# Converting the first four weight tiles by way of SBUF in an attention and feed-forward kernel

## The chip, the cores and the metric

The kernel runs on one core of a Trainium2 chip. The metric is device time in microseconds (us). The engines are TensorE (PE in the rows, with PEld for its weight loads), VectorE (DVE), ScalarE (ACT), GpSimd (POOL) and SyncE (SP), which here only issues transfers.

## What is computed

Attention over 2 batches x 8 heads with rotary position encoding, then two feed-forward layers on its output. In the reference, cut to what matters:

```
q_rot, k_rot = rotate(q), rotate(k)              # (2, 8, 576, 64)
attn = softmax(scale * q_rot @ k_rot^T)
x = (attn @ v) as (1152, 512)                    # tokens x model
h = max(x @ w_in, 0);  y = (h * h) @ w_out       # 512 -> 2048 -> 512
out = ((y @ w_a) * (y @ w_b)) @ w2_out           # 512 -> 1536 -> 512
```

The weights arrive as 64-bit floats and are turned into 32-bit values inside the kernel.

## The kernel before

The 16 heads are worked in 8 pairs. A pair is 9 score tiles (`emit_S`, L205): each is 128 rows of queries against 576 keys. VectorE takes the row maximum of a score tile (L214), ScalarE the exponential (L220), PE transposes the result (L275), and some steps later PE multiplies it with v (`av`, L312 and L317). There are two score tiles in PSUM, so PE can make one score tile while the one before is being read. Beside this, each pair rotates the q and k of the next pair (`prepare`, L154 to L157, on VectorE and GpSimd together) and moves them to their places with transfers from SyncE's queue (`sk`, L142). The result of a pair is scaled and split into a high and a low half (L330, L333, L334) into `xb`, three blocks of 384 tokens.

The feed-forward layers run as units. `unit1(f, n)` is twelve matmuls (`three`, L391 to L393, for four slices of the model dimension): high half of the weight with high half of x, high with low, low with high. The first twelve units need the w_in tiles 0 to 3, called i0 to i3 here; then come i4 and the w_out tiles o0 to o3.

`prep_weight` makes one weight tile out of 64-bit floats. A transfer brings `raw` (two buffers). ScalarE writes `cl` (L77, L78), VectorE works on it in place (L79, L80) and joins it with the low words of `raw` to `bits` (L81); ScalarE rounds `bits` to the high half (L83), and GpSimd subtracts to get the low half (L84). The tiles go round 14 buffers: the first ones of each round lie in the pool `wa`, which exists from the start, the others in the pool `wb`, which takes over memory that attention has given back. Before the change, `wa` holds three tiles, and each `cl` lies in PSUM, in the pool `mps` of the feed-forward stage. This pool takes over the banks of attention's pool `ps`:

```python
attn.close()
...
mps.append(ctx.enter_context(tc.tile_pool(name="mps", bufs=6, space=bass.MemoryType.PSUM, reuse_waits="tile")))
```

All eight banks are attention's until then. `prep_weight` is called in program order, after the last line of attention, but a scheduler orders each engine's instructions by their dependences and free buffers, so an instruction can stand earlier in an engine's queue than in the code if what it writes to is free.

Of the kernel before, what the change touches and what calls it, by code (L numbers as in the profile page):

```python
# [26 lines left out]
LT = 3  # L27
DM = 512
NWT = 14
NWA = 3  # L30


@with_exitstack
def attention_moe_moe2_kernel(ctx: ExitStack, tc: tile.TileContext, qk, rope, vm, vt, ident_in, sel_in, w_in, w_out, w_a, w_b, w2_out, out):
# [8 lines left out]
    tmp = ctx.enter_context(tc.tile_pool(name="tmp", bufs=1))  # L43
    wpools = [ctx.enter_context(tc.tile_pool(name="wa", bufs=NWA))]

# [16 lines left out]
    def prep_weight(key):  # L62
        st = raw.tile([P, DM], I64, tag="raw", name=f"raw_{key[0]}{key[1]}")
        nc.sync.dma_start(out=st, in_=src_of[key[0]][key[1]])
        w = wpools[int(len(W) % NWT >= NWA)].tile([P, 2, DM], F32R, tag="w", name=f"w_{key[0]}{key[1]}")
        W[key] = w
        words = st.bitcast(I32).rearrange("p (n two) -> p n two", two=2)
        low = words[:, :, 0]
        highf = st.bitcast(F32).rearrange("p (n two) -> p n two", two=2)[:, :, 1]
        bits = tmp.tile([P, DM], I32, tag="bits", bufs=2, name=f"bits_{key[0]}{key[1]}")  # L70
        if mps:
            cl = mps[0].tile([P, DM], F32, tag="cl", bufs=2, name=f"cl_{key[0]}{key[1]}")
        else:
            cl = tmp.tile([P, DM], F32, tag="cl", name=f"cl_{key[0]}{key[1]}")
        clb = cl.bitcast(I32)

        act.activation(cl, highf, AF.Copy, scale=REBIAS)  # L77
        act.activation(cl, cl, AF.Prelu, alpha=TURN)  # L78
        dve.tensor_scalar(out=cl, in0=cl, scalar1=-HI * TURN, scalar2=HI, op0=ALU.max, op1=ALU.min)  # L79
        dve.tensor_scalar(out=clb, in0=clb, scalar1=3, scalar2=None, op0=ALU.logical_shift_left)  # L80
        dve.scalar_tensor_tensor(out=bits, in0=low, scalar=29, in1=clb, op0=ALU.logical_shift_right, op1=ALU.bitwise_or)  # L81
        val = bits.bitcast(F32)
        act.copy(w[:, 0, :], val)  # L83
        pool.tensor_tensor(out=w[:, 1, :], in0=val, in1=w[:, 0, :].bitcast(F32), op=ALU.subtract)  # L84

    src_of = {"i": w_in, "o": w_out, "a": w_a, "b": w_b, "2": w2_out}
    W = {}

    mps = []
# [291 lines left out]
    gb = ctx.enter_context(tc.tile_pool(name="gb", bufs=1, reuse_waits="tile"))  # L381
    wpools.append(ctx.enter_context(tc.tile_pool(name="wb", bufs=NWT - NWA, reuse_waits="tile")))
    accp = ctx.enter_context(tc.tile_pool(name="accp", bufs=1, reuse_waits="tile"))
# [114 lines left out]
    for fn, *a in steps:  # L498
        if fn is unit1:
            keys = [("i", a[0])]  # L500
        elif fn is unit2:
            keys = [("a", a[0]), ("b", a[0])]
        else:
            keys = [("o" if fn is out1 else "2", a[0] * G + k) for k in range(G)]
        for key in keys:
            if key not in W:
                prep_weight(key)
        fn(*a)
# [66 lines left out]
```

## Time and profile before

| | |
|---|---|
| time, median of 3 runs | 620.53 us (620.43 to 620.54) |
| the profiled execution's own time | 620.49 us |
| its span, first to last instruction | 618.7 us |
| busy: PE, PEld | 584.4 us (94%), 521.7 us (84%) |
| busy: DVE, ACT, POOL | 333.9 (54%), 322.1 (52%), 255.2 us (41%) |
| attention | from the start to about 180 us |
| feed-forward layers | from about 186 us to the end |

Busy shares are averages over stages with different limits. The ends of matmuls are modelled, so a stretch in which PE is fully busy is one in which its starts follow without a gap, not one at its peak.

### The profile page before, as it was taken

Reading aid. Unit: us, or ns where it says so; the run is one execution under the profiler, and the core shown is the slowest. Engines: PE = TensorE matmul, PEld = TensorE weight load, DVE = VectorE, ACT = ScalarE, POOL = GpSimd, SP = SyncE. Lnnn points to the kernel's source line nnn. Section 1 sums busy time; section 2 is a strip of 40 time slices with the busy share of each in tenths; the row PEclk is TensorE's granted clock in tenths of the full one; section 3 lists DMA queues with packets and bytes.
Section 4 is the critical chain, followed back from the end, with each engine's and each line's share of the span. In section 5 each row is a group of like instructions: output and inputs, shape, how many; then the busy total and the mean of one; then the engine's idle time right before and its main releaser. Section 6 shows DMA issues by size and latency. Waiting matters only on the chain.

```text
span 618.7 us, 8930 instructions
## 1 busy us (share of the span) xinstructions
PE 584.4 (94%) x3368; PEld 521.7 (84%) x3368; DVE 333.9 (54%) x550; ACT 322.1 (52%) x685; POOL 255.2 (41%) x278
## 2 busy tenths in 40 slices
PE   0699999999968999999999999999999999999998
PEld 0567666776637999999999999999988999889986
DVE  5977667754434766777675376764440553221122
ACT  2577777766635877774682356564452653102200
POOL 4567655521214863672561334444331534202210
PEclk9999999999987999999999999999999999999999
DMA  7675765550003344444341222232320440000012
GB/s 231 186 198 140 210 181 157 116 115 4 17 1 136 137 137 136 137 137 137 117 133 57 68 69 103 79 126 77 123 75 1 136 136 1 0 1 1 1 52 102
DMA packets 20678, 61.41 MB, mean 99 GB/s; under 512 B 3337, under 2 KB 3721, under 8 KB 19739
## 3 DMA queue, kind: packets, MB, share of 16 engines
q1 hardware_dynamic: 20635, 60.85, 32.3%
q8 instruction: 26, 0.43, 0.3%
q14 instruction: 17, 0.14, 0.1%
HBM read 48.16 MB, written 2.36 MB: 82 GB/s over the span
## 4 chain that ended last, share of the span: by engine, by line
PE 91%; DVE 5%; ACT 1%; DMA 1%; issue 1%; POOL 0%; SPq 0%; DVEq 0%; ACTq 0%
PE s L205 8%; PE av L317 7%; PE h L393 6%; PE h L391 5%; PE h L392 5%; PE y L391 5%; PE y L392 5%; PE y L393 5%; PE t L275 5%; PE a L392 4%; PE b L392 4%; PE a L393 4%; PE b L393 4%; PE a L391 4%; PE b L391 4%; PE o L467 4%
## 5 line engine op out<-in xcount | busy, mean ns | idle before, releaser
L411 POOL TENSOR_TENSOR g<-v,g 128x384 fp32r<-128x384 f32 x84 | 85.3, 1018 | 136.7 <-ACT g L410 129.9
L205 PE MATMUL s<-sk 128*128 128x288 f32 x336 | 65.1, 322 | 20.5 <-DVE sk L183 15.0
L205 PEld LDWEIGHTS s<-sk 128*128 128x128 f32 x336 | 48.5, 195 | 40.3 <-ACT P L220 15.0
L410 ACT CAST g<-v 128x384 fp32r<-128x384 f32 x84 | 42.9, 510 | 58.7 <-DVE v L409 58.1
L391 PE MATMUL h<-x,w_i 128*128 128x384 f32 x192 | 65.5, 341 | 7.3 <-ACT w_i L83 7.3
L214 DVE TENSOR_REDUCE st<-s 128x1 f32<-128x576 f32 x72 | 53.6, 751 | 34.6 <-PE s L205 34.4
L393 PE MATMUL h<-x,w_i 128*128 128x384 f32 x192 | 65.5, 341 | 1.1 <-POOL w_i L84 1.1
L392 PE MATMUL h<-x,w_i 128*128 128x384 f32 x192 | 65.1, 339 | 0.0
L391 PE MATMUL y<-g,w_o 128*128 128x384 f32 x192 | 64.1, 334 | 0.0
L392 PE MATMUL y<-g,w_o 128*128 128x384 f32 x192 | 64.1, 334 | 0.0
L393 PE MATMUL y<-g,w_o 128*128 128x384 f32 x192 | 64.1, 334 | 0.0
L220 ACT ACTIVATE P<-s,st 128x576 f32<-128x576 f32 x72 | 53.6, 745 | 11.3 <-DVE st L214 11.1
L391 PE MATMUL a<-yb,w_a 128*128 128x384 f32 x144 | 48.1, 334 | 0.0
L393 PE MATMUL a<-yb,w_a 128*128 128x384 f32 x144 | 48.1, 334 | 0.0
L392 PE MATMUL a<-yb,w_a 128*128 128x384 f32 x144 | 48.1, 334 | 0.0
L392 PE MATMUL b<-yb,w_b 128*128 128x384 f32 x144 | 48.1, 334 | 0.0
L393 PE MATMUL b<-yb,w_b 128*128 128x384 f32 x144 | 48.1, 334 | 0.0
L391 PE MATMUL b<-yb,w_b 128*128 128x384 f32 x144 | 48.1, 334 | 0.0
L317 PE MATMUL av<-PT,V 128*64 128x384 f32 (+1 forms) x256 | 48.0, 425 | 0.0
L409 DVE TENSOR_TENSOR v<-b,s 128x384 f32<-128x384 f32 x36 | 19.9, 553 | 50.3 <-PE b L393 50.3
L275 PE MATMUL t<-ident,P 128*128 128x128 f32 x288 | 45.6, 280 | 1.1 <-DVE PT L260 0.8
L391 PEld LDWEIGHTS h<-x,w_i 128*128 128x128 f32 x192 | 36.9, 192 | 8.0 <-ACT w_i L83 8.0
(118 smaller groups left out, 1340.9 us busy)
## 6 DMA issues: line engine op xcount, KB each, us to landing
raw_i<-in_w_in SPq DMA_DIRECT2D x16, 512.0 KB, 3.3
raw_o<-in_w_out SPq DMA_DIRECT2D x16, 512.0 KB, 3.3
X<-in_qk SPq DMA_DIRECT2D x7, 1152.0 KB, 5.3
raw_a<-in_w_a SPq DMA_DIRECT2D x12, 512.0 KB, 3.2
raw_b<-in_w_b SPq DMA_DIRECT2D x12, 512.0 KB, 3.3
raw<-in_w_out SPq DMA_DIRECT2D x12, 512.0 KB, 3.4
sk<-hi_lo SPq DMA_DIRECT2D x14, 432.0 KB, 5.7
sk<-hi_lo SPq DMA_DIRECT2D x14, 288.0 KB, 5.9
```

Source lines behind the costliest of these rows:

```text
L205: pe.matmul(s[:, b, c:c + n], lhs, rhs, start=(m < 2), stop=(m >= len(mm) - len(cuts)), skip_group_check=(j == 8))
L214: dve.tensor_reduce(out=ST[p][:, 0, j:j + 1], in_=SP[i][:, :, 0:288], op=ALU.max, axis=AX.XY, negate=True)
L220: act.activation(pr[:, h, :].rearrange("p (b n) -> p b n", b=2), SP.pop(i)[:, :, 0:288], AF.Exp, bias=st[:, 0, j:j + 1], scale=1.0, accum_ ...
L275: pe.transpose(t[:, k * P:(k + 1) * P], flat[:, c0:c0 + P], ident)
L317: pe.matmul(AVT[p, r][half(h), 0:n], V[p][:, h, k, :], PT[p][:, h, k, q0:q0 + n], start=False, stop=(k == 3), skip_group_check=True)
L391: pe.matmul(dst, wh, mh, start=first, stop=False)
L392: pe.matmul(dst, wh, ml, start=False, stop=False)
L393: pe.matmul(dst, wl, mh, start=False, stop=last)
L409: dve.tensor_tensor(out=val, in0=src, in1=other, op=ALU.mult)
L410: act.copy(gt[:, 0, c], val)
L411: pool.tensor_tensor(out=gt[:, 1, c], in0=val, in1=gt[:, 0, c].bitcast(F32), op=ALU.subtract)
L467: pe.matmul(dst, gt[:, 1, c], w[:, 0, d], start=False, stop=(k == G - 1))
```

## The change

The pool `wa` gets four tiles in place of three (so `wb` gets ten in place of eleven), and while the first four tiles are made, `cl` is a tile of the SBUF pool `tmp`, with one buffer, in place of a PSUM tile. `W` has the new key in it already when the test is reached, so its length is 1 to 4 for i0 to i3. All later tiles use PSUM as before.

```diff
-NWA = 3
+NWA = 4
...
         bits = tmp.tile([P, DM], I32, tag="bits", bufs=2, name=f"bits_{key[0]}{key[1]}")
-        if mps:
+        if len(W) > NWA:
             cl = mps[0].tile([P, DM], F32, tag="cl", bufs=2, name=f"cl_{key[0]}{key[1]}")
         else:
             cl = tmp.tile([P, DM], F32, tag="cl", name=f"cl_{key[0]}{key[1]}")
```

With that, the four conversions move in the queues of the engines. On PE, at the end of attention and the start of the first unit (`av7` is the last pair's product, `h0_0` the first unit's result, in brackets what an instruction waits for), before (-) and now (+):

```order
 L250 MATMUL r7_1_1889<-rows7_1_1891,sel_78 128x64
 L317 MATMUL av7_1_1896<-PT7_1670,V7_1731 64x192 x5
-L391 MATMUL h0_0_1941<-x0_80,w_i0_1931 128x384 [waits Activation_49]
+L391 MATMUL h0_0_1941<-x0_80,w_i0_1931 128x384
 L392 MATMUL h0_0_1941<-x0_80,w_i0_1931 128x384
-L393 MATMUL h0_0_1941<-x0_80,w_i0_1931 128x384 [waits Pool_49]
+L393 MATMUL h0_0_1941<-x0_80,w_i0_1931 128x384
```

The matmuls stand where they stood; the waits for ScalarE's high half and GpSimd's low half of i0 are gone.

On ScalarE, where pair 2 ends and pair 3 begins (`P3_0` is the first exponential of pair 3, `cl_i0` belongs to tile i0):

```order
 L220 ACTIVATE P2_4_701,st2_497<-s26_657,st2_497 128x576
 L258 COPY xf1_1_800<-r1_1_689 128x192
+L77 ACTIVATE cl_i0_1933<-raw_i0_1929 128x512
 L258 COPY PT2_570<-t23_704 128x4x128
+L78 ACTIVATE cl_i0_1933<-cl_i0_1933 128x512
 L220 ACTIVATE P3_0_720,st3_719<-s27_696,st3_719 128x576
 L258 COPY PT2_570<-t24_723 128x4x128
```

The first two steps of tile i0 have moved from the end of attention to this place, ahead of pair 3's exponentials.

On VectorE, early in pair 4 (`s37` to `s39` are its second to fourth score tiles, `cl_i1` belongs to tile i1):

```order
 L214 TENSOR_REDUCE st4_941<-s37_936 128x1
+L260 COPY PT3_792<-t34_962 128x4x128
 L214 TENSOR_REDUCE st4_941<-s38_955 128x1
-L260 COPY PT3_792<-t34_962 128x4x128
+L79 TENSOR_SCALAR cl_i1_1965<-cl_i1_1965 128x512
+L260 COPY PT3_792<-t35_994 128x4x64
+L80 TENSOR_SCALAR cl_i1_1965<-cl_i1_1965 128x512
 L214 TENSOR_REDUCE st4_941<-s39_986 128x1
 L330 TENSOR_TENSOR xf2_1_1022<-av2_1_932,xf2_1_1022 128x192
-L260 COPY PT3_792<-t35_994 128x4x64
```

Two steps of tile i1 now stand between two row maxima, and two copies have moved up. Tile i2 stands likewise in pair 5, and tile i3 at the end of pair 5. On SyncE the loads of i2, i3, i4 and o0 have moved from behind attention's last load to places among the loads and moves of pairs 5 to 7.

## Rows read from the trace of the kernel before

**Rows 1.** Busy us and instructions of each engine by stretch, clock, DMA share, GB/s.
```profile
core 0: us, PE busy (x) PEld busy (x) DVE busy (x) ACT busy (x) POOL busy (x), PEclk, DMA share, GB/s
...
72.00:90.50 18.50, 18.50 (x129) 12.92 (x128) 12.86 (x24) 13.73 (x34) 11.53 (x14) 1.00 0.69 188
90.50:111.00 20.50, 20.12 (x129) 13.60 (x128) 16.25 (x23) 13.66 (x34) 13.45 (x16) 1.00 0.54 145
111.00:129.50 18.50, 18.26 (x127) 12.71 (x126) 12.21 (x24) 13.63 (x35) 8.21 (x15) 1.00 0.42 94
...
148.00:166.50 18.50, 18.50 (x129) 12.94 (x127) 10.29 (x21) 12.72 (x34) 3.25 (x12) 1.00 0.06 17
220.00:300.00 80.00, 80.00 (x463) 80.00 (x463) 54.20 (x89) 53.06 (x104) 41.52 (x37) 1.00 0.42 137
```

**Rows 2.** What PE waited for: us in total, times, longest us.
```profile
PE h L391 <- ACT w_i L83: 7.3, 2, 6.2
```

**Rows 3.** PE's timeline at the boundary (start, us, what, idle before), and its stretch.
```profile
179.07 1.19 PE L317 MATMUL av<-PT,V 128*64 128x192 f32 x10
186.47 0.69 PE L391 MATMUL h<-x,w_i 128*128 128x384 f32 x1 [6.21 <-ACT w_i L83]
...
188.31 0.52 PE L391 MATMUL h<-x,w_i 128*128 128x384 f32 x1
...
192.47 0.39 PE L392 MATMUL h<-x,w_i 128*128 128x384 f32 x1
...
195.16 0.45 PE L391 MATMUL h<-x,w_i 128*128 128x384 f32 x1 [1.09 <-ACT w_i L83]
...
198.74 0.45 PE L393 MATMUL h<-x,w_i 128*128 128x384 f32 x1
199.02 0.34 PE L391 MATMUL h<-x,w_i 128*128 128x384 f32 x1
...
186.50:198.80 12.30, 10.13 (x39) 8.80 (x39) 4.92 (x8) 6.13 (x12) 7.00 (x6) 0.75 0.46 154
```

**Rows 4.** Stretches before and after PE's idle time, columns as in rows 1.
```profile
178.00:180.30 2.30, 2.26 (x20) 1.40 (x19) 0.24 (x2) 0.92 (x3) 1.14 (x2) 1.00 0.00 0
...
189.00:191.00 2.00, 2.00 (x8) 2.00 (x7) 0.03 (x1) 1.21 (x2) 0.00 (x0) 0.50 0.44 174
```

**Rows 5.** The chain that ended last, in order of time, behind attention's end.
```profile
181.11 1.06 ACT cl_i L77 x2
```

**Rows 6.** Groups by form: busy us, mean ns of one, idle before and its releasers.
```profile
L77 ACT ACTIVATE cl_i<-raw_i 128x512 f32<-128x512 f32 x16 | 10.0, 632 | 7.1 <-DMA raw_i<-in_w_in 7.1
L78 ACT ACTIVATE cl_i<-cl_i 128x512 f32<-128x512 f32 x16 | 9.2, 581 | 0.3
L83 ACT CAST w_i<-bits_i 128x512 fp32r<-128x512 f32 x16 | 9.9, 617 | 6.9 <-DVE bits_i L81 6.7
L79 DVE TENSOR_SCALAR cl_i<-cl_i 128x512 f32<-128x512 f32 x16 | 11.0, 696 | 12.4 <-ACT cl_i L78 12.4
L81 DVE SCALAR_TENSOR_TENSOR bits_i<-raw_i,cl_i 128x512 int32<-128x512 int32 x16 | 10.8, 682 | 0.7
L84 POOL TENSOR_TENSOR w_i<-bits_i,w_i 128x512 fp32r<-128x512 f32 x16 | 20.5, 1286 | 27.1 <-ACT w_i L83 27.1
L154 POOL TENSOR_TENSOR X<-X,cs_rot 128x1152 f32<-128x1152 f32 x6 | 18.6, 3097 | 0.0
```

**Rows 7.** The row maximum on VectorE, columns as in rows 6.
```profile
L214 DVE TENSOR_REDUCE st<-s 128x1 f32<-128x576 f32 x72 | 53.6, 751 | 34.6 <-PE s L205 34.4
```

**Rows 8.** Timelines of DVE and POOL in pair 4.
```profile
91.36 2.51 DVE L155 TENSOR_TENSOR cs_rot<-X 128x576 f32<-128x576 f32 x1
93.79 1.37 DVE L234 TENSOR_SCALAR st<-st 128x3 f32<-128x3 f32 x1
...
90.63 2.62 POOL L154 TENSOR_TENSOR X<-X,cs_rot 128x1152 f32<-128x1152 f32 x1
93.33 1.81 POOL L155 TENSOR_TENSOR cs_rot<-X 128x576 f32<-128x576 f32 x1
```

## The prediction

> **What bounds the kernel now.** I read four views: the busy table cut by stage, the waits of the matmul engine PE, its timeline where attention ends and the feed-forward stage begins, and the other engines' rows in that place and in attention.
>
> The stage table shows PE without a gap in the attention pairs that nothing disturbs (18.50 us busy of 18.50, in the stretches 72 to 90.5 and 148 to 166.5) and in the feed-forward stage (80.00 of 80.00) [rows 1]. So a microsecond that PE loses inside either stage is a microsecond of the span, and one that another engine loses is not, as long as its queue stays ahead of PE. VectorE and ScalarE are busy 12.86 and 13.73 us of such an 18.5 us pair. The exception is pair 4, the stretch 90.5 to 111: it takes 20.50 us.
>
> PE's list of waits has one large entry outside the start-up: 7.3 us in two pieces for ScalarE's L83, the high half of a converted w_in tile [rows 2]. The timeline places them. The last attention matmul ends at 179.07 + 1.19 = 180.26 us; PE then sits idle for 6.21 us until 186.47, starts, runs slowly, stops again for 1.09 us before 195.16, and only from 199.02 on do its starts follow each other evenly [rows 3]. The granted clock is 1.00 (2.4 GHz) up to 180.30 and 0.50 (1.2 GHz) at 189 to 191, after the idle stretch [rows 4]. What PE waits for is a chain that begins only when attention's last copy is through: ScalarE starts L77 on the first tiles at 181.11 [rows 5], though their bytes were in SBUF long before; `cl` lies in a bank of the feed-forward stage's PSUM pool, and those banks are attention's until then.
>
> **What the change removes.** In the changed order the first projection matmul carries no wait at all, and it stands right behind the last attention matmul; the waits for tiles i0 to i3 are gone, because all four are converted in pairs 3 to 5. What remains before h1_0 is one wait on ScalarE, and all that ScalarE has before the conversions at this place is over by 181.11, while h1_0 starts twelve matmuls after 180.26.
>
> Its worth: the table counts 39 matmuls from the first one (186.47) to 198.74, so the start at 199.02 is the fortieth [rows 3]. At the feed-forward pace, 80.00 us / 463 = 0.1728 us each [rows 1], 39 of them take 6.74 us. Without the gap the fortieth starts at 180.26 + 6.74 = 187.00, that is 12.02 us sooner. In this sum are 6.21 and 1.09 us of idle time, and 1.91 us of low clock in the stretch 188.31 to 192.47 alone (13 starts at 4.16 / 13 = 0.32 us in place of 0.173); the other 2.8 us are the waits for the low halves and the slow first matmuls behind each stop. Nothing of it is given back later, as far as I see: PE is busy without a gap from there on [rows 1], and tiles i4 and o0 are now loaded ahead as well, so their conversions can begin at about 181, and the first one is needed after twelve units of twelve matmuls (180.26 + 144 x 0.1728 = 205.1). Bounds: 12.0 if the clock stays at 1.00, as it does as long as PE works [rows 1, 4]; 9.1 if some 20 matmuls still run at 0.32 instead of 0.173.
>
> **What it adds in attention.** The instructions are the same; they stand elsewhere. Each tile brings ScalarE L77, L78 and L83 (0.63 + 0.58 + 0.62 = 1.83 us), VectorE L79, L80 and L81 (0.70 + 0.70 + 0.68 = 2.08, with L80 taken as L79) and GpSimd L84 (1.29) [rows 6]. Pairs 3 and 4 take one tile each, pair 5 two. For pair 3 that is 15.6 us of ScalarE and 14.9 of VectorE in 18.5, so PE stays the bound by the totals. By place, VectorE's row maximum L214 has 34.4 us in which it waited for PE's scores over the 72 tiles, about half a microsecond each [rows 7]; one conversion instruction in front of it (0.6 to 0.7) is mostly taken up there, since PE has a second score tile to work on. In pair 3 the ScalarE row order shows L77 and L78 ahead of the first exponentials, 1.2 us; PE has transposes and `av` matmuls moved forward to fill that, and I put it at nothing (bounds 0 and 1.2). In pair 5 one tile falls where VectorE is free and the other delays one maximum: 0.3. Pair 4 is the one that runs late already, and there L79 and L80 both stand ahead of a maximum: I take one of the two, 0.7, with bounds of nothing and both plus a GpSimd wait, 1.4 + 2.6.
>
> The gain side has an unknown as well: pair 4's extra 2.0 us come from a collision that the new order may shift. VectorE's L155 at 91.36 takes 2.51 us and ends at 93.87, 0.62 us after GpSimd's L154 (90.63 + 2.62 = 93.25) ends; its tiny L234 at 93.79 takes 1.37 and ends with GpSimd's L155 (93.33 + 1.81 = 95.14) [rows 8]. If the shifted rows miss each other, 2.0 us come back; I do not count on it, because both still start from the same transfers.
>
> By these rows, then, VectorE and GpSimd shut each other out on some instructions over SBUF tiles, and this speaks against the change: with `cl` in SBUF, L79, L80 and L81 join that group. The Trainium skill, "SBUF — State Buffer", section "Who interferes with whom", states it as a rule: a VectorE instruction with at most one SBUF input and no two-port mode does not contend with GpSimd, one with two SBUF inputs or a two-port `tensor_scalar` does, and the loser blocks for the whole instruction. The rows above agree (2.51 and 1.37 us, both ending with GpSimd's work); no row here shows a large `tensor_scalar` from SBUF. What it would do is a rival below.
>
> SyncE: the loads of i2, i3, i4 and o0 move up into attention's queue, behind the pair loads and ahead of later `sk` moves. Each waits for an L81, two tiles back. The `sk` moves behind them belong to the next pair and start late in the current one, after its L81, so I cost this at nothing; if an L81 slipped by a whole pair, the moves and then the next pair's scores would slip too.
>
> **The sum.** The profiled execution: span 618.70, time 620.49, so 1.79 us lie around the span; the median of three is 620.53, no different. 620.49 - 12.0 + 0.7 + 0.3 = 609.5 us.
>
> **Rivals.**
> *The lock costs more than a microsecond.* GpSimd is busy 11.53, 13.45 and 8.21 us in pairs 3 to 5, 58% of 57.5 us [rows 1]. Twelve VectorE instructions, 58% of them hit, each waiting about 1.5 us (the 1.9 and 1.2 that the two rows lost): 10.4 us, and 8.3 of their own. VectorE's idle time there is 18.50 - 12.86, 20.50 - 16.25 and 18.50 - 12.21, 16.2 in all. So 2.5 us stick out, and unlucky places add as much: 2.5 to 6 on the path, 611 to 614.5, say 612.5. For it: pair 4. Against it: many of the new rows stand where GpSimd has only the short instructions of the softmax scale.
> *Slower than before.* The same lock with every hit on the longest kind, GpSimd's L154 at 3.10 us [rows 6]: 12 x 3.10 + 8.3 = 45.5 us against 16.2 idle, 29 on the path, 637. It decides from (16.2 + 12.0 - 8.3) / 12 = 1.66 us per instruction on; L154 runs once a pair, so three hits are possible, not twelve.
> *Attention gets shorter too.* Pair 4's collision goes away and nothing is paid: 620.49 - 12.0 - 2.0 = 606.5.
> *The gap is filled by another wait.* The change would not do what it says if h0_0 met a late `xb` tile or a late bank. The order shows no wait at it, and attention's copies are through by 181.11. With half of the 6.21 us left, and the 1.91 us of low clock behind it, 609.5 + 3.1 + 1.9 = 614.5; if all of it stays and attention pays, 621.5.
>
> **How the numbers follow.** Likeliest, 0.70: the gap closes and attention pays between nothing and two microseconds and a half, 609.5, own range 608.5 to 611. Lock, 0.14: 612.5. Shorter, 0.10: 606.5. Other wait, 0.03: 614.5, or 621.5 in a third of these. Slower, 0.03: 637. For eight in ten I go from 606.5 to 613.5. A measurement of this kernel can tell about 0.2% (1.2 us) from no change. Faster by more: 0.70 + 0.14 + 0.10 + 0.02 = 0.96; the same 0.01; slower 0.03.
>
> **What would show it.** In the profile after: PE's 6.21 us entry for ScalarE L83 gone, the first h matmul within 0.3 us of the last `av` one, the clock at 1.00 across it, 0.17 us starts from the first unit on. L77 to L84 for `cl_i` in three stretches between about 72 and 131. Pair periods of 18.5 us in pairs 3 and 5, and 20 to 22 in pair 4. I would be wrong if PE shows new waits for ScalarE L220 of more than 2 us in pairs 3 to 5, if L79 to L81 show durations well over 1 us beside GpSimd's L154, L155 or L157, or if the second to fourth unit wait for a bank.

## The result, and the profile after

| | before | after |
|---|---|---|
| time, median of 4 runs each | 620.48 us (619.85 to 620.54) | 613.94 us (613.54 to 614.29) |
| profiled execution's span | 618.70 us | 611.8 us |
| last attention matmul ends | 180.26 us | 184.10 + 1.19 = 185.29 us |
| fortieth feed-forward matmul starts | 199.02 us | 192.09 us |
| from there to the end of the span | 419.68 us | 419.71 us |

The medians differ by 6.5 us, where 11.0 were forecast. The recorded ratio is 0.9882, with a 95% interval of [0.9863, 0.9901]; on 620.5 us that is 7.3 us less, a time of 613.2; why it is not the ratio of the two medians (0.9895) is not on record. The predicted 609.5 us was 4.4 us too low by the medians; they put the result 0.4 us above the upper end of the range, 613.5, and the ratio puts it 0.3 us below.

The table splits the difference of the spans. From the end of attention to the fortieth feed-forward matmul it took 199.02 - 180.26 = 18.76 us and takes 192.09 - 185.29 = 6.80, so 11.96 us are won. Attention ends 5.03 us later. Behind the boundary 0.03 us are lost. -11.96 + 5.03 + 0.03 = -6.9.

The boundary in PE's timeline of the changed kernel answers to [rows 3] (start, us, what, idle before):

```profile
184.10 1.19 PE L317 MATMUL av<-PT,V 128*64 128x192 f32 x10
185.22 0.44 PE L391 MATMUL h<-x,w_i 128*128 128x384 f32 x1
185.50 0.34 PE L392 MATMUL h<-x,w_i 128*128 128x384 f32 x1
...
192.09 0.33 PE L391 MATMUL h<-x,w_i 128*128 128x384 f32 x1
```

Its stretch by engines answers to the last of [rows 3] and to [rows 4] (the granted clock is the third figure from the end):

```profile
185.30:191.90 6.60, 6.60 (x38) 6.60 (x39) 4.53 (x9) 4.30 (x10) 1.75 (x3) 1.00 0.00 0
```

The 6.21 us of idle time are gone, the starts follow each other at 0.17 us from the second matmul on, and the clock stays at 1.00. The boundary is as forecast. PE's whole list of waits in the changed kernel (us in total, times, longest) answers to [rows 2]:

```profile
PE s L205 <- DVE sk L183: 15.0, 1, 15.0
PE s L205 <- ACT P L220: 5.1, 2, 4.0
PE t L275 <- DVE PT L260: 2.2, 2, 1.3
PE r L250 <- DVE rows L260: 1.4, 2, 1.0
PE t L275 <- ACT PT L258: 0.2, 1, 0.2
```

No entry for a weight tile is left. But the list does not explain 5 us either: between 45 us and the end of attention PE waited 1.3 us for a copy and 0.5 for `rows`; the rest is the start-up.

So I cut attention into pairs, from the start of one pair's last score tile (the only one of ten matmuls) to the next one's, and looked at the matmuls of the `av` tile alone. Columns: stretch, its length, busy us and instructions of PE, of its weight loads and of VectorE, clock, DMA share, GB/s. Pairs 3 to 6 of the kernel before, a cut that [rows 1] do not have:

```profile
69.28:87.79 18.51, 6.51 (x38) 2.38 (x36) 0.90 (x2) 1.00 0.69 189
87.79:108.27 20.48, 8.20 (x38) 3.03 (x36) 0.91 (x2) 1.00 0.54 145
108.27:127.10 18.83, 6.51 (x38) 2.38 (x36) 0.91 (x2) 1.00 0.43 95
127.10:145.66 18.56, 6.50 (x38) 2.38 (x36) 0.91 (x2) 1.00 0.43 96
```

and of the changed kernel:

```profile
69.29:88.84 19.55, 7.92 (x38) 2.74 (x36) 0.92 (x2) 1.00 0.64 179
88.84:110.71 21.87, 8.68 (x38) 2.84 (x36) 0.91 (x2) 1.00 0.58 160
110.71:132.19 21.48, 9.05 (x38) 3.21 (x36) 0.92 (x2) 1.00 0.51 132
132.19:150.69 18.50, 6.50 (x37) 2.38 (x36) 0.91 (x2) 1.00 0.53 125
```

Pairs 3, 4 and 5 take 1.04, 1.39 and 2.65 us more. In the same pairs the same 38 `av` records take 1.41, 0.48 and 2.54 us more of PE. The clock is 1.00 in all of them, and nothing was added to PE.

The rows of the whole engines in the same stretches (busy us of PE, PEld, DVE, ACT and POOL) split the difference. Pairs 4 and 5 before, then after:

```profile
87.79:108.27 20.48, 20.10 (x129) 13.58 (x127) 16.14 (x23) 13.66 (x34) 12.06 (x15) 1.00 0.54 145
108.27:127.10 18.83, 18.59 (x130) 13.04 (x128) 13.32 (x23) 13.68 (x34) 9.80 (x14) 1.00 0.43 95
```

```profile
88.84:110.71 21.87, 20.57 (x130) 13.39 (x128) 17.24 (x26) 15.58 (x38) 12.66 (x15) 1.00 0.58 160
110.71:132.19 21.48, 21.03 (x130) 13.77 (x128) 17.74 (x26) 16.83 (x40) 14.57 (x16) 1.00 0.51 132
```

PE has no idle time in pair 3, before or after. Over the three pairs it is busy 61.15 us in place of 57.20 and idle 1.75 in place of 0.62. So of the 5.08 us, 3.95 are longer work of PE itself and 1.13 are waits.

PE's timeline shows what makes the work longer. The eight matmuls of one `av` tile half at 384 columns are four steps, in each the 64 columns of head 0 and then those of head 1 (L317). In the kernel before they stand in two runs of four (each such matmul leaves two records):

```profile
122.84 1.51 PE L317 MATMUL av<-PT,V 128*64 128x384 f32 x8
...
125.66 1.51 PE L317 MATMUL av<-PT,V 128*64 128x384 f32 x8
127.10 1.07 PE L205 MATMUL s<-sk 128*128 128x288 f32 x7
```

and at the same place of the changed kernel:

```profile
124.48 0.86 PE L317 MATMUL av<-PT,V 128*64 128x384 f32 x2
125.27 0.22 PE L242 MATMUL r<-ident,part 128*18 128x128 bf16 x1
...
127.01 1.50 PE L317 MATMUL av<-PT,V 128*64 128x384 f32 x6
...
129.60 0.86 PE L317 MATMUL av<-PT,V 128*64 128x384 f32 x2
130.39 0.44 PE L285 MATMUL tk<-ident,P 128*128 128x128 f32 x2
130.75 1.50 PE L317 MATMUL av<-PT,V 128*64 128x384 f32 x6
```

In pair 4 of the changed kernel a run of two stands by itself:

```profile
104.68 0.87 PE L317 MATMUL av<-PT,V 128*64 128x384 f32 x4
105.48 0.53 PE L205 MATMUL s<-sk 128*128 128x288 f32 x2
```

A run of four holds PE for 125.66 to 127.10, 1.44 us. One matmul alone holds it for 124.48 to 125.27, 0.79 us, a run of two for 0.80, and three hold it as long as four. The two heads' matmuls use different halves of the array's columns and run side by side if they follow each other; where a transpose or a score matmul stands between them, each takes the time of a pair. The Trainium skill, "TensorE: Matmul & The Clock Gate", section "Part 3: Packing small matmuls — row/col tiling", says that such matmuls run concurrently in one array; the runs of four agree, and the runs of one and three show when it does not come about.

From this came two theories of the 5 us. **Order theory:** the scheduler, given the conversions, has put PE's queue into another order that splits `av` steps, three more at 384 columns and three at 192 (one of each in pair 3, two of each in pair 5; pair 4 has no more unpaired matmuls than before, but its `av` matmuls stand in ten runs in place of eight); PE itself takes longer. **Lock theory**, a rival of the prediction: VectorE and GpSimd shut each other out around the conversions, and ScalarE and VectorE carry more, so PE waits.

### The profile page after: what moved, and what is told of

It reads as the page before. It is cut to its first block, busy times and chain, and to the rows that moved or that the text cites. A ratio compares the mean times of both kernels' runs of the same rounds, so it can differ in the third digit from the quotient of the medians.

```text
span 611.8 us, 8929 instructions
## 1 busy us (share of the span) xinstructions
PE 584.6 (96%) x3368; PEld 520.3 (85%) x3368; DVE 333.6 (55%) x550; ACT 321.4 (53%) x685; POOL 257.2 (42%) x278
## 4 chain that ended last, share of the span: by engine, by line
PE 92%; DVE 5%; DMA 1%; issue 1%; ACT 1%; SPq 0%; DVEq 0%; ACTq 0%
PE av L317 8%; PE s L205 7%; PE h L391 5%; PE y L391 5%; PE h L393 5%; PE h L392 5%; PE y L393 5%; PE y L392 5%; PE t L275 5%; PE a L391 4%; PE a L393 4%; PE b L391 4%; PE b L393 4%; PE a L392 4%; PE b L392 4%; PE o L467 4%
## 5 line engine op out<-in xcount | busy, mean ns | idle before, releaser
L391 PE MATMUL h<-x,w_i 128*128 128x384 f32 x192 | 64.2, 335 | 0.0
L392 PE MATMUL h<-x,w_i 128*128 128x384 f32 x192 | 64.1, 334 | 0.0
L393 PE MATMUL h<-x,w_i 128*128 128x384 f32 x192 | 64.1, 334 | 0.0
L220 ACT ACTIVATE P<-s,st 128x576 f32<-128x576 f32 x72 | 53.6, 745 | 13.2 <-DVE st L214 13.0
L317 PE MATMUL av<-PT,V 128*64 128x384 f32 (+1 forms) x256 | 52.4, 425 | 0.0
L467 PE MATMUL o<-w,g 128*128 128x512 f32 (+1 forms) x112 | 42.8, 382 | 0.0
```

Of the source, the lines that this page charges most:

```text
L220: act.activation(pr[:, h, :].rearrange("p (b n) -> p b n", b=2), SP.pop(i)[:, :, 0:288], AF.Exp, bias=st[:, 0, j:j + 1], scale=1.0, accum_ ...
L317: pe.matmul(AVT[p, r][half(h), 0:n], V[p][:, h, k, :], PT[p][:, h, k, q0:q0 + n], start=False, stop=(k == 3), skip_group_check=True)
L391: pe.matmul(dst, wh, mh, start=first, stop=False)
L392: pe.matmul(dst, wh, ml, start=False, stop=False)
L393: pe.matmul(dst, wl, mh, start=False, stop=last)
L467: pe.matmul(dst, gt[:, 1, c], w[:, 0, d], start=False, stop=(k == G - 1))
```

## The experiments

All are timed against the kernel before on the same chip, in 4 to 9 runs each; runs 1 to 4, 5 to 8, 9 to 11 and 12 were on four chips, so medians of different groups compare less well than ratios. Executions differ by up to 2.8 us in when the last score tile of pair 1 starts (48.7 to 51.5 us; runs 12 and 8, with the same order on PE, 48.8 and 51.2), so the table beside the times gives pair lengths.

**Runs 1 to 4: PE's order tied, the other queues free.** A wrapper notes PE's attention instructions as the program emits them, and edges that only fix the order of issue then tie them into a written order (the table is not shown).

```diff
-    act, dve, pool, pe = nc.scalar, nc.vector, nc.gpsimd, nc.tensor
+    act, dve, pool, pe = nc.scalar, nc.vector, nc.gpsimd, InOrder(nc.tensor)
...
+    pe.tie(tc, ORDER)
+    pe = nc.tensor
     attn.close()
```

Run 1, kernel before with the changed kernel's PE order:

> The kernel before, with PE's attention instructions tied by issue-order edges into the order that they have in the changed kernel. The conversions stay at the boundary. Order theory (PE's new order splits the two heads' 64-column av matmuls into runs of odd length, and an unpaired one costs a whole slot: 0.64 us at 384 columns, 0.32 at 192; three more of each): attention ends about 3 us later, 620.5 + 3.2 = 623.7 us. Lock theory (VectorE and GpSimd shut each other out on the conversions, and the loads on VectorE and ScalarE do the rest): no conversion stands in attention, so 620.5 within half a microsecond.

Run 2, changed kernel with the PE order of before:

> The changed kernel, with PE's attention instructions tied into the order that they have in the kernel before; the conversions stay in attention (pairs 3 and 4). Order theory: about 3 us come back, 613.9 - 3.2 = 610.7 us. Lock theory: nothing comes back, 613.9 or more, since the conversions now crowd pair 4.

Run 3, kernel before, heads paired:

> The kernel before, with PE's own attention order, except that the first head's av matmul of each step is put off to stand right ahead of the second head's. Order theory: the kernel before has 5 wasted slots of 384 columns and 6 of 192, 5 x 0.64 + 6 x 0.32 = 5.1 us; where PE is not the bound (pairs 0, 1, 4) some is lost, so 4 to 5: about 616 us. Lock theory: 620.5, the order of these matmuls costs nothing.

PE's queue in the kernel before (-) and paired (+), at the first `av` tile (... stands for other operations):

```
-L317 MATMUL av_0_390<-PT_189,V_226 64x384
...
-L317 MATMUL av_0_390<-PT_189,V_226 64x384
+L317 MATMUL av_0_390<-PT_189,V_226 64x384 x2
...
-L317 MATMUL av_0_390<-PT_189,V_226 64x384
...
-L317 MATMUL av_0_390<-PT_189,V_226 64x384
+L317 MATMUL av_0_390<-PT_189,V_226 64x384 x2
```

Run 4, changed kernel, heads paired:

> The changed kernel with PE's own order and every av step paired in the same way; the conversions stay in attention. Order theory: 8 wasted slots of 384 columns and 9 of 192, 8 x 0.64 + 9 x 0.32 = 8.0 us at the most; with some lost to waits 607 to 608 us. Lock theory: 613.9.

**Runs 5 and 6.** Run 2 turned out unclear: with PE tied, the scheduler moved the conversions too, and three of the four fell into pairs 3 and 4. So from here on all engines' attention parts are tied, as the last step of the program, and only what is named differs.

```diff
         fn(*a)
+    tie(tc, ORDER)
...
+def tie(tc, order):
+    made = {i.name: i for i in tc.nc.cur_bb.bb.instructions}
+    for runs in order.values():
+        names = [f"I-{a + k}" for a, n in runs for k in range(n)]
+        for before, after in zip(names, names[1:]):
+            tc.add_manual_dep(made[after], before, mybir.DependencyInfo(mybir.DependencyClass.NoSync, mybir.DependencyReason.DATA), reason="order")
```

Run 5, the changed kernel with PE alone in the old order:

> The changed kernel with every engine's attention part tied: ScalarE, VectorE, GpSimd and SyncE in the changed kernel's own order, PE alone in the order of the kernel before. The conversions stand exactly where the change put them. Order theory: the 3.7 us that the order alone cost in the first run come back, 613.9 - 3.7 = 610.2 us, with pair periods of about 18.5, 21.4 and 19.3 us in pairs 3 to 5. Lock theory: 613.9, since nothing on VectorE, ScalarE or GpSimd has changed.

Run 6, the same with PE in the changed kernel's order, each first-head matmul moved down to its partner as in run 3:

> The changed kernel with the same ties, PE in its own order but each first-head av matmul put off to the second head's. Order theory: an unpaired av matmul costs 0.79 us at 384 columns (its slot and the restart behind it) and 0.39 at 192; 8 and 9 of them are wasted, 8 x 0.79 + 9 x 0.39 = 9.8 us, 604 us if no other engine becomes the bound, 607 to 610 if the other engines' orders keep part of it. Lock theory: 613.9.

**Runs 7 and 8: the conversions two pairs later.**

VectorE's queue in pair 6, against the kernel before:

```
 L214 TENSOR_REDUCE st_1387<-s_1401 128x1
+L79 TENSOR_SCALAR cl_i_1933<-cl_i_1933 128x512
+L80 TENSOR_SCALAR cl_i_1933<-cl_i_1933 128x512
 L260 COPY PT_1236<-t_1408 128x4x128
 L214 TENSOR_REDUCE st_1387<-s_1432 128x1
+L81 SCALAR_TENSOR_TENSOR bits_i_1932<-raw_i_1929,cl_i_1933 128x512
```

> The changed kernel with PE, ScalarE, VectorE and GpSimd tied into the order of the kernel before, and the four conversions put into pairs 6 and 7, two a pair, where GpSimd has no rotation to do (3.25 us busy of 18.5) and VectorE and ScalarE have 8.2 and 5.8 us free. Order theory: attention takes what it took before and the boundary gap is closed, 620.5 - 12.0 = 608.5 us, at most 0.5 more. Lock theory: the load stays, 3.66 us of ScalarE and about 3.0 of VectorE in each pair, but no GpSimd work to collide with, so 609 to 611.

> The same with PE's av matmuls paired in the order of before. Order theory: the kernel before wastes 5 slots of 384 columns and 6 of 192, 5 x 0.79 + 6 x 0.39 = 6.3 us; 608.5 - 6.3 = 602.2 us if the other engines follow, 604 to 607 if they keep part of it. Lock theory: as the run before, 609 to 611.

**Run 9: four splits, no conversion.** PE's queue in one of the four places, before (-) and now (+):

```
-L275 MATMUL t_1511<-ident,P_1_1437 128x128 x4
-L317 MATMUL av_0_1502<-PT_1236,V_1297 64x384 x4
+L275 MATMUL t_1511<-ident,P_1_1437 128x128 x3
+L317 MATMUL av_0_1502<-PT_1236,V_1297 64x384
+L275 MATMUL t_1511<-ident,P_1_1437 128x128
+L317 MATMUL av_0_1502<-PT_1236,V_1297 64x384 x3
```

> The kernel before with every engine's attention part tied to its own order, and in four places of pairs 6 and 7, where nothing else disturbs, one transpose put between the two heads' first av matmul of a run of four (384 columns). No work is added and no conversion stands near. Order theory: each place costs one slot and one restart, 4 x 0.79 = 3.2 us, in pairs 6 and 7 alone: 620.7 + 3.2 = 623.9 us. Lock theory: 620.7, the order of these matmuls is free.

**Runs 10 and 11: GpSimd's L84 moved.** GpSimd's queue at the start of pair 4's rotation and behind its end:

```
 L157 TENSOR_TENSOR hi_lo<-cs_rot,hi_lo 128x576
-L84 TENSOR_TENSOR w_i_1931<-bits_i_1932,w_i_1931 128x512
 L334 TENSOR_TENSOR x_80<-xf_0_898,x_80 128x384
 L154 TENSOR_TENSOR X_1175<-X_1175,cs_rot 128x2x576
...
 L157 TENSOR_TENSOR hi_lo<-cs_rot,hi_lo 128x576
+L84 TENSOR_TENSOR w_i_1931<-bits_i_1932,w_i_1931 128x512
```

> The fifth run's kernel (changed kernel, PE in the order of before), with the low-half subtractions L84 of tiles i0, i1 and i2 put behind the rotation's last GpSimd instruction L157 of their pair in place of ahead of its L154. VectorE, ScalarE and PE keep their orders. The fifth run paid 2.1 us in pair 4 and 1.0 in pair 5 over the kernel before. If GpSimd's L84 ahead of the rotation makes the VectorE instructions L154 and L155 wait (2.2 and 2.7 us in place of 1.2 and 0.7), most of that comes back: 612.0 - 2 = 610 us. If it is the plain load on VectorE and ScalarE, nothing: 612.0.

> The sixth run's kernel (changed kernel with paired av matmuls, 606.9 us) with the same three L84 moved. If the lock ahead of the rotation is what is left: pairs 4 and 5 fall from 20.9 and 19.7 towards 19 us, 604.5 to 605.5 us. If the load is: 606.9.

**Run 12: run 3 with the other queues held.** PE's order as in run 3, tied as in run 5.

> The third run again (kernel before, av matmuls paired), now with ScalarE, VectorE, GpSimd and SyncE tied to the order of the kernel before, so that PE's order is all that changes. The third run gave 2 us where 4 to 5 were expected, with new waits in pairs 2, 3 and 5. If those came from the other engines' queues, which the scheduler had rearranged: about what pairing gave between the seventh and the eighth run by pairs (1.1 in pair 2, 0.6 in pair 4, 0.2 in pair 5, 1.7 behind pair 7), 620.6 - 3.6 = 617.0 us. If pairing itself makes PE wait there: 619.4 as in the third run.

What was measured (ratio to the kernel before on the run's own chip with its 95% interval; lengths of pairs 2 to 7, and from the last score tile of pair 7 to the end of attention, of the profiled execution):

| | median us | ratio | 2 | 3 | 4 | 5 | 6 | 7 | end |
|---|---|---|---|---|---|---|---|---|---|
| before | 620.48 | | 19.49 | 18.51 | 20.48 | 18.83 | 18.56 | 18.55 | 16.05 |
| after | 613.94 | 0.9882 | 19.49 | 19.55 | 21.87 | 21.48 | 18.50 | 18.56 | 16.04 |
| 1 before, new PE order, rest free | 625.00 | 1.0054 [1.0035, 1.0073] | 19.49 | 19.55 | 20.96 | 20.98 | 18.51 | 18.55 | 16.04 |
| 2 after, old PE order, rest free | 613.61 | 0.9873 [0.9856, 0.9889] | 19.48 | 20.97 | 23.25 | 19.05 | 18.56 | 18.56 | 16.05 |
| 3 before, paired, rest free | 619.41 | 0.9978 [0.9961, 0.9995] | 19.84 | 19.89 | 18.46 | 20.06 | 18.56 | 18.55 | 14.34 |
| 4 after, paired, rest free | 612.00 | 0.9842 [0.9826, 0.9858] | 19.79 | 19.96 | 20.82 | 20.39 | 18.51 | 18.54 | 14.34 |
| 5 after, old PE order | 612.00 | 0.9860 [0.9845, 0.9875] | 19.50 | 18.82 | 22.54 | 19.79 | 18.54 | 18.56 | 16.04 |
| 6 after, paired | 606.86 | 0.9775 [0.9758, 0.9791] | 18.38 | 18.34 | 20.92 | 19.72 | 18.50 | 18.55 | 14.33 |
| 7 conversions late | 610.05 | 0.9821 [0.9804, 0.9837] | 19.49 | 18.50 | 20.47 | 18.83 | 18.54 | 19.09 | 16.04 |
| 8 late and paired | 605.97 | 0.9757 [0.9736, 0.9778] | 18.38 | 18.50 | 19.90 | 18.63 | 18.56 | 19.06 | 14.34 |
| 9 before, four splits | 624.92 | 1.0065 [1.0042, 1.0087] | 19.48 | 18.50 | 20.48 | 18.83 | 20.42 | 20.42 | 16.04 |
| 10 as 5, L84 moved | 609.90 | 0.9818 [0.9797, 0.9840] | 19.49 | 18.85 | 21.68 | 18.85 | 18.56 | 18.55 | 16.04 |
| 11 as 6, L84 moved | 604.50 | 0.9736 [0.9712, 0.9759] | 18.37 | 18.35 | 20.11 | 19.39 | 18.49 | 18.56 | 14.33 |
| 12 before, paired | 616.79 | 0.9936 [0.9905, 0.9966] | 18.38 | 18.51 | 19.90 | 18.65 | 18.54 | 18.56 | 14.33 |

The ties themselves cost nothing that shows: runs 7 and 9, tied into the order of before, repeat its pairs 2 to 5 to 0.02 us.

*Order is a cost of its own: runs 1 and 9.* Run 1 has no conversion in attention, and its pairs 3 to 5 take 1.04, 0.48 and 2.15 us more than before, 3.67 in all. Its `av` rows are those of the changed kernel (same columns):

```profile
70.20:89.75 19.55, 7.93 (x38) 2.74 (x36) 0.92 (x2) 1.00 0.65 179
89.75:110.71 20.96, 8.67 (x38) 2.84 (x36) 0.91 (x2) 1.00 0.54 142
110.71:131.69 20.98, 9.06 (x38) 3.21 (x36) 0.92 (x2) 1.00 0.38 86
```

Run 9 sets the price. Pairs 6 and 7, which take 18.5 to 18.6 us wherever nothing is put into them, grow to 20.42 with two splits each: 0.93 us a split, a little over the 0.79 expected. Its `av` rows for these two pairs, and one of the places in its timeline:

```profile
128.20:148.62 20.42, 8.21 (x38) 2.74 (x36) 0.91 (x2) 1.00 0.38 87
148.62:169.04 20.42, 8.21 (x37) 2.73 (x36) 0.91 (x2) 1.00 0.06 16
```

```profile
142.38 0.86 PE L317 MATMUL av<-PT,V 128*64 128x384 f32 x2
143.17 0.33 PE L275 MATMUL t<-ident,P 128*128 128x128 f32 x1
143.43 1.50 PE L317 MATMUL av<-PT,V 128*64 128x384 f32 x6
```

In run 1 the queues of ScalarE and VectorE moved too, but PE is busy 61.06 us in the three pairs, 3.86 more than before, and idle 0.43, no more than before: the time is PE's own. The lock theory expected nothing in either run. As the only cause it falls.

*But the conversions cost something too: run 5.* With PE in its old order, pairs 3 to 5 still take 0.31, 2.06 and 0.96 us more than before, 3.33 in all; the order theory as the only cause falls as well. Run 5 keeps ScalarE, VectorE and GpSimd in the changed kernel's order, so these 3.33 us are the price of the conversions together with queues that were arranged for another order of PE. PE's order 3.67 and this 3.33 make 7.0, where the change paid 1.04 + 1.39 + 2.65 = 5.08: the two overlap by 1.9 us. A likely reason is that a VectorE that is late costs nothing while PE is busy with its own extra slots; PE idles 3.34 us in these pairs of run 5, and 1.75 in the changed kernel. In pair 4 the two together even cost less than the second alone (1.39 and 2.06). So run 5 got 1.75 us of pair length back (1.9 by the medians), not the 3.7 expected.

*What in the conversions: runs 5 and 10.* VectorE, GpSimd, ScalarE and PE early in pair 4 of run 5, in order of start:

```profile
89.64 1.28 POOL L84 TENSOR_TENSOR w_i<-bits_i,w_i 128x512 fp32r<-128x512 f32 x1 [0.76 <-ACT w_i L83]
89.95 2.19 DVE L154 TENSOR_TENSOR X<-X,cs_rot 128x1152 f32<-128x1152 f32 x1
90.88 2.12 POOL L334 TENSOR_TENSOR x<-xf,x 128x384 fp32r<-128x384 f32 x1
...
92.96 2.64 POOL L154 TENSOR_TENSOR X<-X,cs_rot 128x1152 f32<-128x1152 f32 x1
...
93.52 2.69 DVE L155 TENSOR_TENSOR cs_rot<-X 128x576 f32<-128x576 f32 x1
...
98.41 0.74 ACT L220 ACTIVATE P<-s,st 128x576 f32<-128x576 f32 x1 [2.40 <-DVE st L214]
...
99.29 0.79 PE L205 MATMUL s<-sk 128*128 128x288 f32 x4 [1.24 <-ACT P L220]
```

and VectorE and GpSimd at the same place of run 10, where L84 stands behind the rotation:

```profile
88.94 1.35 DVE L154 TENSOR_TENSOR X<-X,cs_rot 128x1152 f32<-128x1152 f32 x1
89.65 1.50 POOL L334 TENSOR_TENSOR x<-xf,x 128x384 fp32r<-128x384 f32 x1 [1.78 <-ACT x L333]
...
91.11 2.63 POOL L154 TENSOR_TENSOR X<-X,cs_rot 128x1152 f32<-128x1152 f32 x1
91.84 2.51 DVE L155 TENSOR_TENSOR cs_rot<-X 128x576 f32<-128x576 f32 x1
```

In run 5 the low-half subtraction of tile i0 runs when the rotation of the next pair begins. VectorE's L154 takes 2.19 us beside it, in place of 1.35, and GpSimd reaches its own L154 at 92.96; the row maxima behind come late, ScalarE's exponential waits 2.40 us, and PE then 1.24 (1.59 and 0.39 in run 10). Moving three L84 gives pair 4 back 0.86 us and pair 5 0.94. The medians, 612.00 and 609.90 on two chips, say 2.1, as the lock half of the expectation had it.

1.56 us stay with the conversions, 1.20 of them in pair 4. No run was made to split them, but two records speak against the plain load on VectorE or ScalarE. Run 7 has two tiles in pair 6, with the queues otherwise as before, and that pair takes 18.54 us (though there is no rotation beside them). And in pair 4 of run 10, PE's longest wait is for an exponential that stands behind a copy of ScalarE:

```profile
98.69 0.37 ACT L258 COPY PT<-t 128x256 f32<-128x256 f32 x1 [1.05 <-PE t L275]
...
98.96 0.75 ACT L220 ACTIVATE P<-s,st 128x576 f32<-128x576 f32 x1
...
99.85 0.80 PE L205 MATMUL s<-sk 128*128 128x288 f32 x4 [0.62 <-ACT P L220]
```

Its row maximum had been ready since 97.77. In the kernel before the exponential (97.04) comes first and the copy (98.20) after it; the scheduler swapped them when the conversions moved, and run 10 keeps the swap. A second wait, 0.43 us for `rows` at 104.41, follows an L81 of 1.19 us (0.68 for tile i0) beside GpSimd's L157. Together they are 1.05 of the 1.20 us. So the order of ScalarE's queue looks like a third part of the cost, which neither theory had; a run with the two put back was not made.

*Runs 2 to 4, 6 and 12.* Run 3 was expected at 616 and came at 619.4. Run 12, the same PE order with the other queues held, gives 616.79 (617.0 expected): the shortfall of run 3 was the scheduler's rearrangement of the other engines, not the pairing. Run 4 against run 6 (the same PE edit, other queues free or held, 612.00 and 606.86) shows the same. Run 2 is undecided for that reason. Run 6, at 606.86, lies at the end of its 607 to 610 us for order theory and far from the lock theory's 613.9. It shares all queues but PE's with the changed kernel, and pairs 3 to 5 take 58.98 us in it in place of 62.90: pairing alone takes 3.92 us out of them.

*A version that beats both.* Run 11, with the conversions in their new places, the heads paired and L84 behind the rotation, takes 604.50 us (604.5 to 605.5 expected, though pairs 4 and 5 did not come down to 19); run 8, with conversions in pairs 6 and 7, 605.97 (604 to 607 expected if the other engines keep part). Much of what pairing gains was there before the change: in run 12, 1.1 us in pair 2 and 1.7 behind pair 7. Run 7 confirms 12 us for the boundary with attention nearly untouched: pair 7 alone pays, 0.54 us, and the time is 610.05 where 608.5 was expected from the order theory and 609 to 611 from the lock theory, which it does not tell apart.

## Why the prediction was right in one term and wrong in the other

*The boundary, 12.02 us, bounds 9.1 and 12.0:* right, 11.96 measured, and the clock stayed at 1.00. That nothing is given back later held to 0.03 us. SyncE's moved loads cost nothing: PE's list of waits has no entry for `sk` but the start-up's.

*Attention, 1.0 us:* mis-sized, 5.08 us measured. The step that failed is "PE has transposes and `av` matmuls moved forward to fill that, and I put it at nothing". It took the moved `av` matmuls as filler of fixed price ("The instructions are the same; they stand elsewhere"). They are priced by their neighbours: each one torn from its partner costs 0.8 to 0.9 us at 384 columns (0.79 of PE's time by its row, 0.93 us of the pair in run 9). Pair 3, put at nothing (bounds 0 and 1.2), paid 1.04, all of it by order (run 1 has the same 19.55 us). Pair 5, put at 0.3, paid 2.65: 2.15 with PE's order alone (run 1), 0.96 with the rest alone (run 5). Pair 4, put at 0.7 (bounds 0 to 4.0), paid 1.39: 0.48 and 2.06. Of tile i3, counted to pair 5, only L77 and L78 fall there (130.91 and 131.62); the rest stands in pair 6, which pays nothing. The sum with the measured terms is 620.49 - 11.96 + 5.03 + 0.03 = 613.6 us, the profiled execution's 613.54.

Of the signs of being wrong, none showed: PE's list has no wait for L220 in pairs 3 to 5, and no L79 to L81 took more than 1.03 us there. They all watched for waits, and most of the cost was busy time. Only the expected pair lengths told: 19.55 and 21.48 us in pairs 3 and 5 in place of 18.5.

*"Pair 4's extra 2.0 us come from a collision":* only in part. The `av` rows of before show 8.20 us there and 6.51 in pairs 3 and 5: 1.7 us are unpaired matmuls, in the trace of before, and I had not cut it by tile. The collision of [rows 8] is real, but lay mostly behind them: PE idles only 0.38 us in that pair. With the heads paired, pair 4 takes 19.90 us (run 12), 1.4 over the others, and PE waits 1.4 us for one exponential. The rival that would have returned 2.0 us by the collision alone had no such ground.

*The lock rival, 612.5 us, own range 611 to 614.5:* the time falls in its range by luck. All of PE's added waits in the three pairs are 1.13 us, less than the 2.5 to 6 it put on the path; the rest of the 5.08 is PE's own work. Its mechanism exists, but not where it was put. It charged the twelve new VectorE instructions. In the changed kernel L79 and L80 mostly took 0.42 us, shorter than the 0.70 I had carried over from PSUM tiles [rows 6]. L81 took 1.03 and 0.84 us for tiles i2 and i3 in place of 0.68, and one L79 was hit for 0.4 us:

```profile
117.49 1.41 POOL L155 TENSOR_TENSOR cs_rot<-X 128x576 f32<-128x576 f32 x1
...
118.32 0.86 DVE L79 TENSOR_SCALAR cl_i<-cl_i 128x512 f32<-128x512 f32 x1
```

That row agrees with the rule of the Trainium skill, "SBUF — State Buffer", section "Who interferes with whom", that was cited ahead of the run, for a large `tensor_scalar` from SBUF. The larger lock cost that was measured, 1.8 us between runs 5 and 10, came through GpSimd's L84, which the sum had only as an instruction of GpSimd's own: ahead of the rotation it shifts L154 and L155.

What stays open: why the scheduler, given the conversions, splits just these steps; and how the last 1.56 us divide between the conversions and the swapped queues of ScalarE and VectorE.

## What to carry to other kernels

Where a scheduler sets the order, a change on one engine moves the queues of the others: compare each engine's busy time for the same instructions, stretch by stretch and tile by tile, before taking its work as fixed. An engine that shows no gap may still be wasting slots; here, keeping the matmuls that share the array by columns next to each other gained 0.6% in the kernel before (run 12) and 1.1% in the changed one (run 6 against it, 0.9775 and 0.9882). When a moved step ends in an instruction on another engine, cost that instruction where it lands too.

## What the runs showed of the hardware

One matmul on 64 columns of the array, 128x384 in 32-bit floats, without its partner held PE for 0.79 us, a pair of them for 0.80, two pairs for 1.44. The same VectorE operations on 128 x 512 tiles (L79, L80) took 0.42 us from SBUF in the changed kernel, where GpSimd did not hold them up, and 0.70 from PSUM before.
